# Two reorderings while the first half's expert places are found: raw-weight squares go behind a step's weight copy on ACT, and the sums of gathered rows go behind the pair's filling work on DVE

## The chip, the cores and the metric

The kernel runs on one core of one Trainium2 chip. The metric is the device time of one execution in microseconds, as the median of several runs. Five engines work beside each other, each through its own queue in order: PE (matrix multiplies), ACT (activations and copies), DVE (vector work), POOL (here above all the issue of gathers) and SP (issue of DMAs).

## What is computed

Cut to what matters, the reference adds an attention block and a mixture of very many small experts to the input:

```python
xn = layernorm(x)                                   # 2048 tokens x 512
# A: 32 heads of 16 channels with one shared key and value head
q = (xn @ wq).reshape(B, S, H, Dh); k = xn @ wk; v = xn @ wv
p = softmax(q k^T * Dh**-0.5);  A = (p v).reshape(B, S, H * Dh) @ wo
# B: 32 heads find 2 of 4096 experts for each token
q = einsum("nd,dhc->nhc", xn, w_q)                  # 2 x 128 channels per head
s1 = q[..., :dk] @ k1.T;  s2 = q[..., dk:] @ k2.T   # 64 scores each
# the best 2 of s1 and the best 2 of s2 make 4 candidates, the best 2 are kept
g = softmax(top_s)
act = gelu(einsum("nd,nhkd->nhk", xn, u[top_e]))
B = einsum("nhk,nhk,nhkd->nd", g, act, v[top_e])
out = x + A + B
```

## The kernel before, in words

The 2048 tokens are four groups of 512. For the first two groups ("phases" 0 and 1) the expert rows are fetched by gathers, for the last two a dense form is used that the change does not touch.

**The attention drives the order.** After a start of some 120 us, `att_steps` (L1434 on) is called for each of 256 pairs `d` of key blocks and writes out, in this order: the score matmuls of one key block (`sc`, L452) with their exponentials on ACT (`pt`, L459, two activations of 128x1024), the value matmuls of the pair before (`pv`, L469), then `mid()`, then the score matmuls and exponentials of the second key block, then `fill()`. The two `sc` tiles in PSUM are a pair: a score matmul waits until ACT has read the tile two places back.

**`fill()`** takes as much as fits of the thread that finds the places of the experts (`run_scores`, `score_thread`). For each of 8 blocks `c` of four heads this thread (1) forms weights in `wp_make(c)`: four `pw` products (L648), copied by ACT to `wt` (L649), then for each of four `k` four transposes into a tile `pwt`, one ACT activation that writes the high half `wk` (L663 before, L661 after) and one DVE operation that writes the low half (`low`, L664); and (2) scores the four token tiles in `item`: twelve `psc` matmuls (L720), eight MAX on DVE (L733) and four index searches (L740). `pw`, `pwt`, `psc` and a few small products share three PSUM tiles of the tag "x": a new one starts when DVE or ACT has read the tile that leaves.

The raw weights of the block that comes next must have a size factor. `wp_square` (L619, ACT, 128x1024 with an accumulated sum of squares) is called four times for each block, in `wp_make` at `k` = 1 (two), 2 and 3 (one each). The sums of squares go through `wp_factors` (product `pn` on PE, `xw` on ACT, three small DVE operations at L223 to L225 into `cols`), before the next block's copies use them.

**`mid()`** holds the work on gathered rows of phase 0 and 1. A step writes out some 2.6 gathered rows each of:
- dots (L1243, DVE): the row's first half times the token, summed;
- after each fourth dot, a chain of three small DVE operations, `gq` (L1252), `gy` (L1253) and `ga` (L1254), kept in the list `CHAIN`;
- the tanh of such four dots on ACT (`gth<-gy`, L1259), written at the start of the next step's `mid()`, so between the two pairs of exponentials;
- `weigh` (`w`, L1266, DVE), which needs the tanh;
- sums (L1278, DVE, `xa<-g,w,xa`): the row's second half, weighted, added to the token's total. They are written by `go()`, mixed with the chain and with other small work;
- `gathers(4)`, also in `go()`: up to four more gathers (L1231, issued by POOL) into the 12 row buffers that the sums have set free; and stores of finished totals.

In the kernel before `go()` runs inside `mid()`, unless `dense_on[0] == 2`; then it is put in the list `POST_FILL`, which `fill()` runs after `run_scores`, and `CHAIN` is run beforehand, inside `mid()`.

`IDX` holds one entry for each token tile and block whose places are known; phase 0 fills it with `NC * TPH` = 32 entries. In the profile this stretch ends at 356 us.

Of the kernel before, what the change touches and what calls it, by code (L numbers as in the profile page):

```python
# [33 lines left out]
NC = 8  # L34
TPH = GT
# [26 lines left out]
def tile_kernel(ctx, tc, exact, flag, x, wq, wkv, wo, wqT, kT, uv, ub, vb, out):  # L62
# [538 lines left out]
    def wp_load(c, h):  # L601
        n = 4 * c + h
        if n < 2 or n > 7 and (n - 8) % 5 < 2:
            w = big.tile([P, 2, D], F32, name="wqt", tag="wqt", bufs=2)
        elif n < 8:
            w = gtile(F32, (P, 2, D), "wqt")
        else:
            w = late[0].tile([P, 2, D], F32, name="wqt", tag="gy", bufs=3)
        nc.sync.dma_start(w, wqT[4 * c + h].rearrange("(s p) d -> p s d", p=P))
        WC["raw", c, h] = w  # L610
# [4 lines left out]
    def wp_square():  # L615
        n = squared[0]
        squared[0] += 1
        junk = big.tile([P, 2, D], BF16, name="junk", tag="wk", bufs=NWK)
        nc.scalar.activation(junk, WC["raw", n // 4, n % 4], AF.Square, accum_out=squares[:, n % 4:n % 4 + 1])  # L619

    def wp_factors():
        c = factored[0]
        factored[0] += 1
        p = xtile("pn")[:, :1]
        for h in range(4):
            nc.tensor.matmul(p, ones_f, squares[:, h:h + 1], start=h == 0, stop=h == 3)
        x = small.tile([P, 1], F32, name="xw")
        nc.scalar.activation(x, p, AF.Copy, scale=col(K2))
        factors(x.bitcast(I32), col(S_W + c), col(I_W + c))

    def wk_tile():
        return big.tile([P, 2, 512], F16, name="wk", tag="wk", bufs=NWK)

    def wp_make(c):

        wt = [big.tile([P, 2, 512], F32, name="wt", tag="da", bufs=2) for _ in range(2)]
        for h in range(4):
            for n in range(4 * c + h + 1, min(4 * c + h + 5, 4 * NC) if late[0] else 4):
                if ("raw", n // 4, n % 4) not in WC:
                    wp_load(n // 4, n % 4)  # L640
            if c == 2 and h > 1:
                wp_square()
            if c > 2 and h == 1:
                wp_factors()
            w = WC.pop(("raw", c, h))
            p = xtile("pw")
            for s in range(2):
                nc.tensor.matmul(p[s * E:(s + 1) * E, :], kTs[:, s, :], w[:, s, :], start=True, stop=True)  # L648
            nc.scalar.copy(wt[h // 2][:, h % 2, :], p)  # L649
            yield 0.9  # L650
        WC[c] = []
        if c == 2:
            yield 0.05
            wp_factors()
            yield 0.05
        for k in range(KC):
            for _ in range((0, 2, 1, 1)[k] if 1 < c < NC - 1 else 0):
                wp_square()
            p = xtile("pwt")
            for h in range(4):  # L660
                nc.tensor.transpose(p[:, h * P:(h + 1) * P], wt[h // 2][:, h % 2, k * P:(k + 1) * P], ident)  # L661
            wk = wk_tile()
            nc.scalar.activation(wk[:, 0, :], p, AF.Copy, scale=col(S_W + c))  # L663
            low = lambda p=p, wk=wk: nc.vector.scalar_tensor_tensor(wk[:, 1, :], p, col(S_W + c), wk[:, 0, :],  # L664
                                                                    op0=OP.mult, op1=OP.subtract)
            if c == 1 and late[0] is None:
                AFTER.append(low)
            else:
                low()
            WC[c].append(wk)  # L670
            (store if c > 1 else BULK.append)(lambda k=k, wk=wk: nc.sync.dma_start(d_w[c][:, k], raw(wk[:])))
            yield 0.45
# [72 lines left out]
    IDX, G = {}, {}  # L745
# [516 lines left out]
    def weigh(n):  # L1262
        if n not in WT and n < a_ready[0] // SB:
            ga, th = GA.pop(n), TH.pop(n)
            w = small.tile([P, SB], F32, name="w", bufs=3)
            nc.vector.scalar_tensor_tensor(w, th, 1.0, ga, op0=OP.add, op1=OP.mult)  # L1266
            WT[n] = w
# [23 lines left out]
    def dots(to):  # L1291
        while d_next[0] < min(to, NSL):
            dot(d_next[0])
            d_next[0] += 1
# [7 lines left out]
    def tanhs(to):  # L1302
        while a_ready[0] + SB <= to:
            tanh(a_ready[0] // SB)
            a_ready[0] += SB
# [8 lines left out]
    def run(fns):  # L1314
        todo = fns[:]
        fns.clear()
        for fn in todo:
            fn()
# [92 lines left out]
    dense_on, quiet = [0], [0]  # L1411
# [90 lines left out]
    def score_steps(n):  # L1502
        for _ in range(n):
            spent[0] += next(sgen)
# [122 lines left out]
    with tc.manual_schedule(engines=ENGINES):  # L1627
        nc.vector.tensor_copy(PK["mm"][96:128], PK["mm"][:32])
        run(AFTER)
        score_steps(3)  # L1630
        done0 = spent[0] - 5.4
        half = STEPS // 2
        pos, since = 0.0, half
        for d in range(half + 24):


            if dense_on[0] != 0:
                since = d
            if dense_on[0] == 1:
                pos += 2.35 if d < half * 3 // 4 else max(0.0, NSL - pos) / max(half - 3 - d, 1)  # L1640
            else:
                pos += (2.6 if len(IDX) < NC * TPH else 2.45 if 0 <= d - since < 32 else 2.05, 0, 0.25, 1.5, 0.5)[dense_on[0]]

            todo = max(min(int(pos + 0.001), g_next[0]) - d_next[0], 0) if d else 0

            def mid():
                post = POST[:]
                POST.clear()
                for act, _ in post:
                    act()  # L1650
                tanhs(d_next[0])
                room = ROOM - 0.65 * len(ON_ACT) - 0.7 * len(LAST)
                run(ON_ACT)
                ON_ACT.extend(LATER_ACT)
                LATER_ACT.clear()
                run(LAST)
                while PARTS and (room > 0.7 or len(PARTS) > 3):
                    PARTS.pop(0)()
                    room -= 0.75
                LAST.extend(LATER)  # L1660
                LATER.clear()
                rest = BEHIND[:]
                BEHIND.clear()

                dots(d_next[0] + todo - 1)
                if a_ready[0] > a_next[0]:
                    weigh(a_next[0] // SB)
                dots(d_next[0] + 1 if todo > 0 else 0)
                for _, fn in post:
                    fn()  # L1670
                sums = min(a_ready[0] - a_next[0], max(todo, 3) if d < half else 4)
                if dense_on[0] > 2:
                    sums = min(sums, 2)
                if quiet[0] > 0:
                    quiet[0] -= 1
                    sums = 0
                if dense_on[0] == 2:
                    run(CHAIN)

                def go():  # L1680
                    n = sums
                    while rest or CHAIN or n > 0:
                        if n > 0:
                            adds(1)
                            n -= 1
                        elif not rest:
                            run(CHAIN)
                        if CHAIN:
                            CHAIN.pop(0)()
                        if rest:  # L1690
                            rest.pop(0)()
                    gathers(4)

                    for _ in range(1 if d < half - 4 else NT):
                        if OUTS:
                            experts_out(OUTS.pop(0))

                if dense_on[0] == 2:
                    POST_FILL.append(go)
                else:  # L1700
                    go()

            aim = done0 + (FILL - done0) * (d + 1) / half if d < half else 1e6

            def fill():
                run_scores(until=min(aim, spent[0] + MOST))
                run(POST_FILL)

            norm_steps(d)
            att_steps(d, mid, fill)  # L1710
            if d == half - 26 and not exact:
                met_most()
            if d == half - 16 and not exact:
                met_flag()
        flush()
        run(STORES)
        while a_next[0] < NSL:
            dots(NSL)
            run(CHAIN)
            tanhs(d_next[0])  # L1720
            adds(SB)
            run(STORES)
            gathers(NGB)
        assert not OUTS
        run(STORES)
# [42 lines left out]
```

## Time and profile before

| | |
|---|---|
| median of 3 runs | 1788.83 us (1785.12 to 1790.47) |
| the profiled execution, its own time | 1779.54 us |
| span of that execution | 1777.7 us |
| PE busy | 1692.0 us (95%) |
| DVE busy | 1534.4 us (86%) |
| ACT busy | 1329.0 us (75%) |
| POOL busy | 709.5 us (40%) |
| granted clock of PE, mean | 0.991 |

A row of the timeline has the start in us from the start of the span, the duration in us, the engine, the line, the operation with its output and inputs, a count if several are merged, and in square brackets the idle time of the engine just before, with what ended it. Three matmul rows can overlap by some hundredths, since their ends are modelled. A row of a table by stage has the stretch, its length, and for each engine the busy us and the number of instructions, then the granted clock of PE (1.00 is full), the busy share of the DMA engines and GB/s.

### The profile page before, as it was taken

The numbers are of one execution on the slowest core, as the hardware profiler recorded it, in microseconds if no ns is written. First come the engines' busy times: TensorE is split into PE (matmuls) and PEld (weight loads), VectorE is DVE, ScalarE is ACT, GpSimd is POOL, SyncE is SP. The second block draws the span as 40 slices with busy tenths as digits, with TensorE's granted clock in tenths as the row PEclk, the third lists the DMA queues.
The fourth block names the chain that finished last, engine by engine and source line by source line (L and its number), as shares of the span: only waits on it lengthen the run. The fifth ranks groups of instructions, "written<-read, shape, count | busy, mean of one in ns | idle before, by whom it ended". The sixth has DMA issues, their size and how long they took to land.

```text
span 1777.7 us, 34221 instructions
## 1 busy us (share of the span) xinstructions
PE 1692.0 (95%) x11071; PEld 598.4 (34%) x11071; DVE 1534.4 (86%) x5385; ACT 1329.0 (75%) x1793; POOL 709.5 (40%) x983
## 2 busy tenths in 40 slices
PE   7989998999999889999999999999998999999997
PEld 3433333333333333333333333333333333333332
DVE  7648888989999977988998898999999778888894
ACT  6468787867777988888988666666679877777773
POOL 1024454555663103433433356566640124444430
PEclk9999999999999999999999999999999999999999
DMA  7378888999983469999899977877653779999892
GB/s 263 128 243 310 278 297 286 307 335 337 330 277 138 159 214 296 301 309 320 290 350 318 334 271 250 281 265 255 195 183 111 257 235 291 305 324 313 262 313 70
DMA packets 257277, 471.02 MB, mean 265 GB/s; under 512 B 107316, under 2 KB 118596, under 8 KB 257084
## 3 DMA queue, kind: packets, MB, share of 16 engines
q0 software_dynamic: 73728, 268.47, 43.7%
q1 hardware_dynamic: 182940, 199.59, 34.8%
q8 instruction: 89, 1.46, 0.3%
q14 instruction: 104, 0.85, 0.1%
q10 hardware_dynamic: 416, 0.66, 0.1%
HBM read 407.36 MB, written 56.39 MB: 261 GB/s over the span
## 4 chain that ended last, share of the span: by engine, by line
PE 67%; DVE 15%; ACT 6%; issue 2%; DMA 2%; ACTq 0%; SPq 0%; DVEq 0%
PE pv L469 20%; PE psc L720 13%; PE sc L452 12%; PE pout L1109 9%; PE pact L967 8%; ACT pt L459 4%; DVE xa L1278 2%; PE pwo L569 2%; DVE oh L1025 2%; DVE g L1243 2%; DVE i L740 2%; DVE m L733 2%; PE pw L648 1%; DVE obs L1028 1%; DVE obs L1027 1%
## 5 line engine op out<-in xcount | busy, mean ns | idle before, releaser
L459 ACT ACTIVATE pt<-sc 128x1024 f32<-128x1024 f32 x1024 | 990.2, 1026 | 318.6 <-PE sc L452 317.5
L1231 POOL DMA_INDIRECT g<-in_uv_dram,idx x512 | 546.6, 1068 | 866.6 <-DVE xa L1278 429.9
L469 PE MATMUL pv<-pt,vaug 128*32 128x512 f32 x4096 | 497.8, 604 | 0.0
L1278 DVE SCALAR_TENSOR_TENSOR xa<-g,w,xa 128x512 f32<-128x512 f32 x512 | 372.4, 744 | 0.1
L720 PE MATMUL psc<-wk,xt 128*128 128x512 f16 x1536 | 357.7, 381 | 5.1 <-DVE wk L664 5.1
L452 PE MATMUL sc<-qa,kaug 64*128 64x512 f16 x2048 | 323.5, 383 | 37.7 <-ACT pt L459 33.7
L1243 DVE CUSTOM_DVE_ANT_0 g<-g,xa 128x512 f32<-128x512 f32 x512 | 333.8, 681 | 0.0
L720 PEld LDWEIGHTS <-xt 128*128 128x128 f16 x1536 | 141.2, 98 | 202.7 <-issue 54.1
L452 PEld LDWEIGHTS <-kaug 64*128 64x128 f16 x2048 | 82.1, 94 | 375.3 <-issue 369.3
L469 PEld LDWEIGHTS pv<-pt,vaug 128*32 128x32 f32 x4096 | 107.6, 110 | 255.9 <-issue 255.9
L967 PE MATMUL pact<-xt,wk 128*128 128x512 f16 x768 | 181.5, 381 | 0.0
L1109 PE MATMUL pout<-wk,wd 128*128 128x512 f16 x768 | 175.8, 379 | 0.0
L733 DVE MAX8 m<-psc 128x8 f32<-128x64 f32 x1024 | 145.7, 212 | 18.3 <-PE psc L720 18.2
L740 DVE FIND_INDEX8 i<-m,psc 128x8 uint32<-128x128 f32 x512 | 138.4, 285 | 0.0
L1109 PEld LDWEIGHTS <-wd 128*128 128x128 f16 x768 | 73.0, 98 | 92.5 <-issue 7.9
L967 PEld LDWEIGHTS <-wk 128*128 128x128 f16 x768 | 68.9, 98 | 99.5 <-issue 26.3
L1025 DVE TENSOR_TENSOR oh<-io,tr 128x2048 f16<-128x2048 f16 x64 | 77.8, 1216 | 5.1 <-PE pg L1063 4.8
L1182 DVE SCALAR_TENSOR_TENSOR gy<-gy,pact 128x512 f32<-128x512 f32 x60 | 41.0, 683 | 36.3 <-ACT gy L1181 35.6
L1266 DVE SCALAR_TENSOR_TENSOR w<-gth,ga 128x4 f32<-128x4 f32 x128 | 20.5, 160 | 55.8 <-ACT gth L1259 55.6
L1112 DVE SCALAR_TENSOR_TENSOR da<-pout,cols,da 128x512 f32<-128x512 f32 x72 | 53.4, 745 | 14.5 <-PE pout L1109 14.4
L784 POOL CAST fi<-i 128x32 f32<-128x32 uint32 x60 | 12.6, 240 | 106.3 <-DVE i L740 106.3
L918 DVE SCALAR_TENSOR_TENSOR wk<-rw,cols,wk 128x512 f16<-128x512 f32 x64 | 47.3, 743 | 6.5 <-ACT wk L911 6.5
(238 smaller groups left out, 1499.9 us busy)
## 6 DMA issues: line engine op xcount, KB each, us to landing
wk<-dw SPq DMA_DIRECT2D x96, 256.0 KB
wqt<-in_wqT_dram SPq DMA_DIRECT2D x32, 512.0 KB
un<-in_uv_dram SPq DMA_DIRECT2D x16, 1024.0 KB
ds<-wk SPq DMA_DIRECT2D x64, 256.0 KB
gates<-dg SPq DMA_DIRECT2D x64, 256.0 KB
wk<-ds SPq DMA_DIRECT2D x64, 256.0 KB
dg<-gst SPq DMA_DIRECT2D x14, 928.0 KB
dw<-wk SPq DMA_DIRECT2D x32, 256.0 KB
```

Source lines behind the costliest of these rows:

```text
L452: nc.tensor.matmul(p[:, b, :], kaug[o:o + 64, kc * P:(kc + 1) * P], QA[u][o:o + 64, i, :], start=True, stop=True)
L459: nc.scalar.activation(PT[u, kc, i], p, AF.Exp, scale=SCALE)
L469: nc.tensor.matmul(PV[u][32 * j:32 * j + 32, :], vaug[:, kc, :], pt[:, b, :], start=kc == 0, stop=kc == 15)
L720: nc.tensor.matmul(p, XT[kk][:, a, j * P:(j + 1) * P], WC[n_][kk][:, bb, :], start=n == 0, stop=n == 11)
L733: nc.vector.max(m8[:, jb, s // 2, SECOND * (s % 2):][:, :8], p[:, s * E:(s + 1) * E])
L740: nc.vector.max_index(i8[:, jb, h, :8], m8[:, jb, h, :8], p[:, h * P:(h + 1) * P])
L967: nc.tensor.matmul(p, us[:, a, k * P:(k + 1) * P], XT[k][:, c, :], start=n == 0, stop=n == 11)
L1025: nc.vector.tensor_tensor(out=oa, in0=num(P), in1=bc(0, tb, P), op=OP.is_equal)
L1109: nc.tensor.matmul(p, wd[0][:, a, j * P:(j + 1) * P], vs[:, c, :], start=n == 0, stop=n == last)
L1231: nc.gpsimd.indirect_dma_start(out=gt, out_offset=None, in_=uv, in_offset=bass.IndirectOffsetOnAxis(ap=IDX[ph, c, ti][:, s:s + 1], axis=0))
L1243: nc.vector.tensor_tensor_reduce(u, u, XN[TPH * ph + ti], scale=1.0, scalar=0.0, op0=OP.mult, op1=OP.add, accum_out=a[:, i:i + 1])
L1278: nc.vector.scalar_tensor_tensor(acc, v, w[:, i:i + 1], acc, op0=OP.mult, op1=OP.add)
```

## The change

Two places are edited. In `wp_make` the calls of `wp_square` at a step `k` move from ahead of that step's transposes and `wk` activation to just behind the activation. And as long as `IDX` has fewer than 32 entries, `go()` (sums, chain, other small work, gathers, stores of totals) is not run in `mid()` but put in `POST_FILL`, so it is written behind the filling work of the same step. `CHAIN` is not run ahead in this new case: the condition for that stays `dense_on[0] == 2`.

```diff
@@ wp_make
         for k in range(KC):
-            for _ in range((0, 2, 1, 1)[k] if 1 < c < NC - 1 else 0):
-                wp_square()
             p = xtile("pwt")
             for h in range(4):
                 nc.tensor.transpose(p[:, h * P:(h + 1) * P], wt[h // 2][:, h % 2, k * P:(k + 1) * P], ident)
             wk = wk_tile()
             nc.scalar.activation(wk[:, 0, :], p, AF.Copy, scale=col(S_W + c))
+            for _ in range((0, 2, 1, 1)[k] if 1 < c < NC - 1 else 0):
+                wp_square()
@@ mid
-                if dense_on[0] == 2:
+                if dense_on[0] == 2 or len(IDX) < NC * TPH:
                     POST_FILL.append(go)
                 else:
                     go()
```

No instruction is added or taken out. The orders of PE and SP are the same row for row. Those of ACT, DVE and POOL change. On ACT, in the weight forming that the profile of before shows from 182 to 195 us (`pt` are the exponentials, `junk` the squares, `wk` the weight copies, `gth` a tanh), before:

```order
L663 ACTIVATE wk<-pwt,cols 128x512
L619 ACTIVATE junk,squares<-wqt 128x1024 x2
L663 ACTIVATE wk<-pwt,cols 128x512
L459 ACTIVATE pt<-sc 128x1024 x2
L1259 ACTIVATE gth<-gy 128x4
L459 ACTIVATE pt<-sc 128x1024 x2
L619 ACTIVATE junk,squares<-wqt 128x1024
L663 ACTIVATE wk<-pwt,cols 128x512
L619 ACTIVATE junk,squares<-wqt 128x1024
L663 ACTIVATE wk<-pwt,cols 128x512
L459 ACTIVATE pt<-sc 128x1024 x2
```

The same place after:

```order
L661 ACTIVATE wk<-pwt,cols 128x512 x2
L619 ACTIVATE junk,squares<-wqt 128x1024 x2
L459 ACTIVATE pt<-sc 128x1024 x2
L1259 ACTIVATE gth<-gy 128x4
L459 ACTIVATE pt<-sc 128x1024 x2
L661 ACTIVATE wk<-pwt,cols 128x512
L619 ACTIVATE junk,squares<-wqt 128x1024
L661 ACTIVATE wk<-pwt,cols 128x512
L619 ACTIVATE junk,squares<-wqt 128x1024
L459 ACTIVATE pt<-sc 128x1024 x2
```

Each copy stands one or two squares earlier; the same four copies and four squares stand between the same exponentials.

On DVE, at the place that the profile of before shows from 284 to 293 us (`ISA g,act` with `ISA act` is a dot, `xa` a sum, `gq`, `gy`, `ga` the chain, MAX and MAX_INDEX the reading of a finished `psc` tile), before:

```order
L1243 ISA g,act<-g,xa 128x512
L1243 ISA act 128x1
L1278 SCALAR_TENSOR_TENSOR xa<-g,w,xa 128x512
L1252 SCALAR_TENSOR_TENSOR gq<-act 128x4
L1278 SCALAR_TENSOR_TENSOR xa<-g,w,xa 128x512
L1253 SCALAR_TENSOR_TENSOR gy<-gq,act 128x4
L1278 SCALAR_TENSOR_TENSOR xa<-g,w,xa 128x512
L1254 TENSOR_TENSOR ga<-act,gg 128x4
L733 MAX m_3473<-psc 128x8 x8
L740 MAX_INDEX i_3474<-m_3473,psc 128x8 x4
L664 SCALAR_TENSOR_TENSOR wk<-pwt,cols,wk 128x512 x2
L1243 ISA g,act<-g,xa 128x512
```

and after:

```order
L1243 ISA g,act<-g,xa 128x512
L1243 ISA act 128x1
L733 MAX m_3461<-psc 128x8 x8
L740 MAX_INDEX i_3462<-m_3461,psc 128x8 x4
L664 SCALAR_TENSOR_TENSOR wk<-pwt,cols,wk 128x512 x2
L1278 SCALAR_TENSOR_TENSOR xa<-g,w,xa 128x512
L1252 SCALAR_TENSOR_TENSOR gq<-act 128x4
L1278 SCALAR_TENSOR_TENSOR xa<-g,w,xa 128x512
L1253 SCALAR_TENSOR_TENSOR gy<-gq,act 128x4
L1278 SCALAR_TENSOR_TENSOR xa<-g,w,xa 128x512
L1254 TENSOR_TENSOR ga<-act,gg 128x4
L1243 ISA g,act<-g,xa 128x512
```

The reading of `psc` and the two low halves come ahead of the three sums; the chain with `gy`, from which ACT's next tanh reads, comes behind them.

## The prediction

> **What bounds the kernel now.** I read the page first, then the table of the stretch that the change reaches, PE's timeline there, the granted clock around its gaps, and then ACT and DVE at the same places. From the page:
>
> ```profile
> span 1777.7 us, 34221 instructions
> PE 1692.0 (95%) x11071; PEld 598.4 (34%) x11071; DVE 1534.4 (86%) x5385; ACT 1329.0 (75%) x1793; POOL 709.5 (40%) x983
> PE 67%; DVE 15%; ACT 6%; issue 2%; DMA 2%; ACTq 0%; SPq 0%; DVEq 0%
> ```
>
> PE carries the chain of waits, so an edit that leaves PE's order alone, as this one does, can only change how long PE stands still. The table of the stretch in which phase 0's places are found (us, then PE, PEld, DVE, ACT, POOL busy, granted clock, DMA share):
>
> ```profile
> 131.00:356.00 225.00, 211.73 (x1299) 74.51 (x1300) 193.09 (x865) 179.30 (x262) 109.63 (x153) 0.98 0.87 297
> ```
>
> PE lacks 225.00 - 211.73 = 13.3 us here, 0.75% of the span: the most that waits can give. DVE has 32 us to spare, ACT 45.7. Of the 13.3 us 11.7 stand in these rows of PE's timeline (idle time in brackets):
>
> ```profile
> 152.18 0.39 PE L452 MATMUL sc<-qa,kaug 64*128 64x512 f16 x2 [1.21 <-ACT pt L459]
> 185.76 1.46 PE L720 MATMUL psc<-wk,xt 128*128 128x512 f16 x6 [0.92 <-DVE wk L664]
> 194.43 2.15 PE L720 MATMUL psc<-wk,xt 128*128 128x512 f16 x6 [1.96 <-DVE wk L664]
> 228.50 0.39 PE L452 MATMUL sc<-qa,kaug 64*128 64x512 f16 x2 [1.05 <-ACT pt L459]
> 261.62 0.81 PE L720 MATMUL psc<-wk,xt 128*128 128x512 f16 x3 [1.01 <-DVE wk L664]
> 291.26 0.63 PE L661 MATMUL pwt<-ident,wt 128*128 128x128 f32 x4 [2.35 <-DVE i L740]
> 300.30 1.48 PE L648 MATMUL pw<-wqt,kTs 128*64 128x512 f32 x4 [2.36 <-issue]
> 324.33 0.81 PE L720 MATMUL psc<-wk,xt 128*128 128x512 f16 x3 [0.88 <-DVE wk L664]
> ```
>
> Behind three of these gaps the granted clock falls (columns: stretch, length, PE busy, clock, DMA share, GB/s):
>
> ```profile
> 154.00:156.00 2.00, 2.00 (x9) 0.52 0.81 315
> 156.00:158.00 2.00, 2.00 (x8) 0.63 0.04 13
> 194.00:196.00 2.00, 1.57 (x6) 0.76 0.86 278
> 196.00:198.00 2.00, 2.00 (x10) 0.50 0.96 348
> 300.00:302.00 2.00, 1.70 (x6) 0.71 0.88 311
> 302.00:304.00 2.00, 2.00 (x12) 0.50 0.82 252
> ```
>
> The lost clock is (0.48 + 0.37 + 0.24 + 0.50 + 0.29 + 0.50) x 2 us = 4.8 us, 1.6 us for each dip. The gap of 2.35 us at 291 has no dip behind it, so a gap of about two microseconds brings one sometimes.
>
> [...]
>
> **The change part by part.** *Squares behind the copy.* ACT and DVE around the gap at 194.43:
>
> ```profile
> 191.86 1.06 ACT L619 ACTIVATE junk<-wqt 128x1024 bf16<-128x1024 f32 x1
> 192.90 0.69 ACT L663 ACTIVATE wk<-pwt,cols 128x512 f16<-128x512 f32 x1
> 192.55 0.15 DVE L1254 TENSOR_TENSOR ga<-act,gg 128x4 f32<-128x4 f32 x1
> 193.62 0.75 DVE L664 SCALAR_TENSOR_TENSOR wk<-pwt,cols,wk 128x512 f16<-128x512 f32 x1 [0.92 <-ACT wk L663]
> ```
>
> The copy waits 1.04 us for a square whose result nobody needs yet; DVE's low half waits for the copy, and PE for the PSUM tile that the low half frees. Behind the change the copy starts at 191.86 and, with the sums (the last with `ga` at 192.55) out of DVE's way, the low half at 193.62 - 1.04 = 192.6: I take 1.1 us of the 1.96. Ahead of the gaps at 261.62 and 152.18 stand these:
>
> ```profile
> 259.06 1.06 ACT L619 ACTIVATE junk<-wqt 128x1024 bf16<-128x1024 f32 x1
> 147.88 0.69 ACT L663 ACTIVATE wk<-pwt,cols 128x512 f16<-128x512 f32 x1 [1.79 <-DVE cols L225]
> ```
>
> The first is again a square ahead of a copy, with its low half and PE behind: 0.8 of 1.01 us, since DVE comes a little later there. In the second ACT waits 1.79 us for `cols`, which moves ahead of three sums on DVE, so the exponentials that PE waits for come sooner: 0.9 of 1.21 us. At 185.76 and 324.33 neither a square nor a sum is in front, and the gaps stay. The work of ACT between two pairs of exponentials is as much as before, so the gap at 228.50 stays too. The squares themselves are read by `pn` steps later; a microsecond there is nothing.
>
> *Sums behind the fill.* PE and DVE ahead of the gap at 291.26, and DVE ahead of that at 300.30:
>
> ```profile
> 286.35 0.82 PE L720 MATMUL psc<-wk,xt 128*128 128x512 f16 x3
> 286.70 0.75 DVE L1278 SCALAR_TENSOR_TENSOR xa<-g,w,xa 128x512 f32<-128x512 f32 x1
> 288.10 0.15 DVE L1253 SCALAR_TENSOR_TENSOR gy<-gq,act 128x4 f32<-128x4 f32 x1
> 288.91 1.14 DVE L733 MAX8 m<-psc 128x8 f32<-128x64 f32 x8
> 298.00 1.14 DVE L733 MAX8 m<-psc 128x8 f32<-128x64 f32 x8
> ```
>
> `psc` is finished at 287.1, but its reading starts at 288.91, since three sums with the chain (286.70 to 288.91) are first. Behind the change it starts at 287.1: 1.8 us of the 2.35 go. At 298.00 the same, less what DVE is later there because the sums of the step before now stand behind its reading: I take 1.6 of 2.36. PE's gaps shrink by 1.1 + 0.8 + 0.9 + 1.8 + 1.6 = 6.2 us. Of the dips I give back half, 2.4 of 4.8 us, since some gap is left at each place; the ends are 0 and 4.8.
>
> *The new wait.* The chain moves with the sums, and ACT's tanh, which reads `gy`, does not. A step with its rows on PE, DVE and ACT:
>
> ```profile
> 164.05 1.47 PE L720 MATMUL psc<-wk,xt 128*128 128x512 f16 x6
> 165.21 0.17 DVE L1253 SCALAR_TENSOR_TENSOR gy<-gq,act 128x4 f32<-128x4 f32 x1
> 165.94 1.94 ACT L459 ACTIVATE pt<-sc 128x1024 f32<-128x1024 f32 x2 [1.19 <-PE sc L452]
> 167.69 0.67 DVE L1243 CUSTOM_DVE_ANT_0 g<-g,xa 128x512 f32<-128x512 f32 x1
> 167.77 0.21 ACT L1259 ACTIVATE gth<-gy 128x4 f32<-128x4 f32 x1
> ```
>
> Today `gy` is there 2.4 us before ACT comes to the tanh. `psc` is finished only at 165.5, so the reading can't come sooner; behind it, from 167.69, stand a sum, `gq`, a sum and `gy`, 1.6 us by the rows quoted above (286.70 to 288.10 + 0.15). The tanh then starts at 169.3 and ACT has waited 1.5 us, with the second pair of exponentials queued behind. The groups of all these tanhs and of the exponentials in the stretch, with their idle time:
>
> ```profile
> L1259 ACT ACTIVATE gth<-gy 128x4 f32<-128x4 f32 x19 | 4.0, 210 | 0.0
> L459 ACT ACTIVATE pt<-sc 128x1024 f32<-128x1024 f32 x122 | 118.2, 1025 | 27.2 <-PE sc L452 27.0
> ```
>
> None of the 19 tanhs waits today; 19 x 1.5 = 28.5 us of ACT's time is the most. The 122 exponentials are those of 30 steps. In a light step ACT has the room (45.7 us idle, 1.5 for each step). It has little in the steps with squares, two in each of five blocks: 10 of 30 steps, with 19 x 10/30 = 6.3 tanhs. Of each wait ACT's usual gap ahead of a pair of exponentials, 27.2/61 = 0.45 us, takes its part, and 6.3 x 1.05 = 6.7 us pass to PE. The ends are 0 (DVE reads `psc` so early that `gy` is in time) and 14 us (half of all waits pass). That a held-up ACT stops PE is seen once in the trace, at 384:
>
> ```profile
> 382.80 1.06 ACT L1379 ACTIVATE un<-un 128x1024 f32<-128x1024 f32 x1 [4.17 <-DMA un<-in_uv_dram]
> 383.85 3.75 ACT L459 ACTIVATE pt<-sc 128x1024 f32<-128x1024 f32 x4
> 384.91 0.39 PE L452 MATMUL sc<-qa,kaug 64*128 64x512 f16 x2 [2.36 <-ACT pt L459]
> ```
>
> 4.17 us of waiting became 2.36 us of PE's.
>
> *Gathers* are issued by POOL half a step later, with their sums. I cost that at nothing: 12 buffers hold more than two steps of rows, and the dots, on the whole kernel, never waited for one (idle 0.0):
>
> ```profile
> L1243 DVE CUSTOM_DVE_ANT_0 g<-g,xa 128x512 f32<-128x512 f32 x512 | 333.8, 681 | 0.0
> ```
>
> If that cover went, the idle time of this group would show it, and half a step of delay, about 3 us, is the most for one row.
>
> **The sum.** -6.2 - 2.4 + 6.7 = -1.9 us: the profiled execution would come to 1779.54 - 1.9 = 1777.6 us. It lay 9.3 us under the median of the runs; the same step from the median is 1786.9 us. About 0.3%, 5.4 us, is what a measurement of this kernel can tell from no change.
>
> **The rivals.** *The tanh's wait is hidden.* For it speaks ACT's idle time of 45.7 us, and that DVE, which today stands before `w` until the tanh is done, then has the reading of `psc` to do; against it, that the copies of the next weights follow on ACT. The gain would be 6.2 + 2.4 = 8.6 us: 1780.2, faster.
>
> *The tanh's wait wins.* ACT, held at each tanh, gives its exponentials late, and PE stands at `sc`. With 14 us passed on, 6.2 us of gaps gone and no dip saved it is 1788.83 + 7.8 = 1796.6, slower. It decides as soon as more than 6.2 + 2.4 + 5.4 = 14.0 us pass, or 11.6 if the dips stay. For it speaks that all 19 tanhs get the new wait; against it, that 20 of 30 steps have room.
>
> *The gain is swallowed at 384.* ACT waits there for rows that a DMA brings. If their landing does not move with PE, the 1.9 us are spent there: 1788.8. Against it speaks that the load is issued in PE's rhythm.
>
> *The dips do not hang on these gaps.* Then the clock falls elsewhere in the same measure and only waits count: -6.2 + 6.7 = 0.5, 1789.3. Against it speaks that each of the three dips begins at a gap; for it, that the gap at 291 brought none. [...]
>
> **How the numbers follow.** My forecast has 0.40, swallowed 0.08, dips independent 0.08: together 0.56 within 0.3% of the median. Tanh hidden has 0.30, the chance of faster; tanh wins 0.14, the chance of slower. The range runs from 1778 (hidden, and nearly all the clock back: 6.2 + 4.6 = 10.8 us) to 1794 (9.5 us passed on, half of the gaps' and the dips' share had: 9.5 - 3.1 - 1.2 = 5.2 us), which leaves out the far ends of both rivals.
>
> **What would show it.** In the profile after: the gaps at 194, 291 and 300 shrunk under 1.2 us, those at 186 and 324 as they were; a new row "ACT gth waits for DVE gy" with 10 to 28 us over some 19 tanhs; PE's wait for `pt` in the stretch grown by some 4 to 8 us; and one or two dips instead of three. I am wrong if `gth` does not wait, if the long gaps stay, or if the time moves outside 131 to 356 us by more than a few microseconds.

## The result, and the profile after

The changed kernel takes 1806.04 us (median of 6 runs, 1800.83 to 1810.18), the kernel before 1788.24 us (median of 6 runs beside it). The ratio is 1.0113, with a 95% interval of 1.0092 to 1.0133: about 20 us slower. Ratios here leave out single slow executions, among them one of 2418.94 us of the kernel before in this comparison and one of 5813.61 us in an experiment below. The forecast was 1786.9 us, no change, with a range that ended at 1794.

The profiled execution of the changed kernel took 1810.18 us, the slowest of its six. Two groups of its page stand out against before, where the dots' group (L1243) had an idle time of 0.0 and the score matmuls' group (L452) waited 33.7 us for `pt`:

```profile
span 1808.5 us, 34225 instructions
PE 1701.8 (94%) x11071; PEld 600.1 (33%) x11071; DVE 1537.2 (85%) x5385; ACT 1327.7 (73%) x1793; POOL 715.8 (40%) x983
PE 61%; DVE 17%; ACT 7%; issue 4%; DMA 2%; another core or an unknown queue 1%; SPq 1%; ACTq 0%; DVEq 0%
...
L452 PE MATMUL sc<-qa,kaug 64*128 64x512 f16 x2048 | 327.9, 384 | 59.5 <-ACT pt L459 47.5
...
L1243 DVE CUSTOM_DVE_ANT_0 g<-g,xa 128x512 f32<-128x512 f32 x512 | 335.0, 683 | 17.1 <-DMA g<-in_uv_dram,idx 14.5
```

PE's share of the chain of waits fell from 67% to 61%, and PE is busy for only 10 us more in a span that is 31 us longer: the rest is PE standing still. The page's groups are of the whole kernel. The stretch of the change holds the same work as 131 to 356 us before (122 exponentials, 19 tanhs) when it is read from 131 to 372 us. Its row of the table by stage, and then its groups:

```profile
131.00:372.00 241.00, 215.57 (x1301) 75.78 (x1297) 194.56 (x867) 178.63 (x262) 114.06 (x156) 0.97 0.83 280
```

```profile
L1259 ACT ACTIVATE gth<-gy 128x4 f32<-128x4 f32 x19 | 4.0, 208 | 22.1 <-DVE gy L1253 11.3 <-DVE gg L815 6.5 <-issue 4.2
L1243 DVE CUSTOM_DVE_ANT_0 g<-g,xa 128x512 f32<-128x512 f32 x78 | 51.2, 687 | 14.5 <-DMA g<-in_uv_dram,idx 14.5
L452 PE MATMUL sc<-qa,kaug 64*128 64x512 f16 x240 | 39.6, 389 | 15.8 <-ACT pt L459 9.9 <-issue 3.3 <-DMA xt<-dxt 2.6
L720 PE MATMUL psc<-wk,xt 128*128 128x512 f16 x345 | 86.8, 387 | 4.6 <-DVE wk L664 4.6
L1266 DVE SCALAR_TENSOR_TENSOR w<-gth,ga 128x4 f32<-128x4 f32 x19 | 2.9, 153 | 0.9 <-ACT gth L1259 0.9
```

The stretch grew by 241 - 225 = 16 us. PE is idle for 241.00 - 215.57 = 25.4 us of it, before 13.3: 12.1 us more. The tanhs wait 22.1 us (before 0.0), the dots 14.5 us for rows that a DMA brings (before 0.0), and PE's idle time ahead of `sc` went from 3.5 to 15.8 us. PE's gaps of over 0.8 us, where eight stood before:

```profile
175.62 0.39 PE L452 MATMUL sc<-qa,kaug 64*128 64x512 f16 x2 [1.77 <-issue]
177.06 0.39 PE L452 MATMUL sc<-qa,kaug 64*128 64x512 f16 x2 [1.05 <-issue]
189.06 1.46 PE L720 MATMUL psc<-wk,xt 128*128 128x512 f16 x6 [0.92 <-DVE wk L664]
196.72 1.45 PE L720 MATMUL psc<-wk,xt 128*128 128x512 f16 x6 [0.96 <-DVE wk L664]
231.62 0.39 PE L452 MATMUL sc<-qa,kaug 64*128 64x512 f16 x2 [2.88 <-ACT pt L459]
258.66 0.81 PE L720 MATMUL psc<-wk,xt 128*128 128x512 f16 x3 [0.87 <-DVE wk L664]
307.47 1.98 PE L648 MATMUL pw<-wqt,kTs 128*64 128x512 f32 x4 [3.50 <-issue]
331.71 0.81 PE L720 MATMUL psc<-wk,xt 128*128 128x512 f16 x3 [1.30 <-DVE wk L664]
353.94 0.39 PE L452 MATMUL sc<-qa,kaug 64*128 64x512 f16 x2 [1.26 <-ACT pt L459]
363.57 0.47 PE L452 MATMUL sc<-qa,kaug 64*128 64x512 f16 x2 [2.59 <-DMA xt<-dxt]
```

The gap at 291 is down to 0.67 us and those at 152 and 194 shrank. In their place stand gaps at `sc`, where PE waits for the exponentials, and the gap of 2.36 us at 300 has become 3.50. How the largest wait of a tanh comes about, in the timeline of POOL, DVE, ACT and PE:

```profile
351.81 1.18 POOL L1231 DMA_INDIRECT g<-in_uv_dram,idx  x1 [0.30 <-DVE ga L1254]
...
356.36 0.69 DVE L1243 CUSTOM_DVE_ANT_0 g<-g,xa 128x512 f32<-128x512 f32 x1 [4.10 <-DMA g<-in_uv_dram,idx]
356.98 1.15 DVE L733 MAX8 m<-psc 128x8 f32<-128x64 f32 x8
...
359.76 0.16 DVE L1252 SCALAR_TENSOR_TENSOR gq<-act 128x4 f32<-128x4 f32 x1
...
361.18 0.15 DVE L1253 SCALAR_TENSOR_TENSOR gy<-gq,act 128x4 f32<-128x4 f32 x1
...
361.37 0.21 ACT L1259 ACTIVATE gth<-gy 128x4 f32<-128x4 f32 x1 [4.74 <-DVE gg L815]
...
362.52 2.83 ACT L459 ACTIVATE pt<-sc 128x1024 f32<-128x1024 f32 x3
...
363.57 0.47 PE L452 MATMUL sc<-qa,kaug 64*128 64x512 f16 x2 [2.59 <-DMA xt<-dxt]
```

A dot waits 4.10 us for its row, the reading of `psc` follows it, and only behind the reading and two sums comes `gy`. The tanh waits 4.74 us for it; behind the tanh stand another activation of 1.04 us (`un`, L1379) and then the exponentials, and PE is idle until the first of these has read its tile (the profile names a DMA as the releaser of 363.57; an experiment below makes the same gap with ACT alone). Of the three longest waits of a tanh only this one has a late row ahead of it; the next two, 2.77 us at 351 and 2.19 us at 224, have none. The pair of gaps at 175 and 177 us has no releaser that the profile names and no waiting tanh just ahead; its cause stays open.

Where the profiled execution falls behind before, by the start of ACT's copies of `pv` (L477, one for each unit of attention; the start after less the start before):

| start before, us | 175 | 236 | 295 | 353 | 511 | 857 | 1118 | 1758 |
|---|---|---|---|---|---|---|---|---|
| after | +2.2 | +4.5 | +5.9 | +15.2 | +19.5 | +19.7 | +28.6 | +31.3 |
| squares alone | -1.0 | -3.6 | -1.9 | -1.9 | -3.7 | -4.0 | -5.3 | -5.0 |

By 511 us 19.5 us are lost, near the difference of the medians (17.8 us). The steps that follow later are no part of it: the step between 1066 and 1118 us also stands, with 3 to 4 us, in two controls below that are no slower than before, and executions of the changed kernel lie up to 9 us apart. So verdicts come from ratios, and a profile says where PE stands.

### The profile page after: what moved, and what is told of

It is laid out like the page before. It is cut to its first block, busy times and chain, and to the rows that moved or that the text cites. A ratio compares the mean times of both kernels' runs of the same rounds, so it can differ in the third digit from the quotient of the medians.

```text
span 1808.5 us, 34225 instructions
## 1 busy us (share of the span) xinstructions
PE 1701.8 (94%) x11071; PEld 600.1 (33%) x11071; DVE 1537.2 (85%) x5385; ACT 1327.7 (73%) x1793; POOL 715.8 (40%) x983
## 4 chain that ended last, share of the span: by engine, by line
PE 61%; DVE 17%; ACT 7%; issue 4%; DMA 2%; another core or an unknown queue 1%; SPq 1%; ACTq 0%; DVEq 0%
PE pv L469 18%; PE sc L452 11%; PE psc L720 11%; PE pout L1109 8%; PE pact L967 8%; ACT pt L459 5%; DVE xa L1278 3%; PE pwo L569 2%; DVE i L740 2%; DVE m L733 2%; DVE g L1243 2%; DVE oh L1025 2%; PE pw L648 1%; DMA xt<-dxt 1%
## 5 line engine op out<-in xcount | busy, mean ns | idle before, releaser
L452 PE MATMUL sc<-qa,kaug 64*128 64x512 f16 x2048 | 327.9, 384 | 59.5 <-ACT pt L459 47.5
L1243 DVE CUSTOM_DVE_ANT_0 g<-g,xa 128x512 f32<-128x512 f32 x512 | 335.0, 683 | 17.1 <-DMA g<-in_uv_dram,idx 14.5
L452 PEld LDWEIGHTS <-kaug 64*128 64x128 f16 x2048 | 83.9, 94 | 406.4 <-issue 398.0
L1112 DVE SCALAR_TENSOR_TENSOR da<-pout,cols,da 128x512 f32<-128x512 f32 x72 | 53.5, 747 | 14.5 <-PE pout L1109 12.7
```

Of the source, the lines that this page charges most:

```text
L452: nc.tensor.matmul(p[:, b, :], kaug[o:o + 64, kc * P:(kc + 1) * P], QA[u][o:o + 64, i, :], start=True, stop=True)
L1243: nc.vector.tensor_tensor_reduce(u, u, XN[TPH * ph + ti], scale=1.0, scalar=0.0, op0=OP.mult, op1=OP.add, accum_out=a[:, i:i + 1])
```

## Theories

T: ACT, held at the tanh by a late `gy`, gives its exponentials late, and PE pays at `sc`. That is the rival "the tanh's wait wins" of the prediction, at a higher price. G: gathers, issued half a step later, bring their rows late, and dots that wait for them hold up what stands behind them on DVE. The prediction costed that at nothing.

## The experiments

Ratios are to the kernel before, measured beside each; the intervals are 95%.

**Squares alone** (the first half of the diff).

> Only the squares go behind the copies; the sums, the chain and the gathers stay where they are in the kernel before. Theory T (the time is lost because the tanh on ACT waits for gy, and the exponentials stand behind it) and theory G (the time is lost because gathers are issued half a step later, so that dots on DVE wait for rows) both put the loss on the other edit. Both expect 0.997 to 1.001 of the kernel before, dots idle 0.0, no tanh that waits for gy. A ratio over 1.004 would put part of the loss on the squares, against both.

Measured: 0.9997 (0.9976 to 1.0019). The gap at 194 shrank from 1.96 to 0.95 us and the one at 261 fell under 0.7, as forecast for these two; less than 2 us is too little to be seen in the time.

```profile
192.40 1.46 PE L720 MATMUL psc<-wk,xt 128*128 128x512 f16 x6 [0.95 <-DVE wk L664]
```

**Sums alone** (the second half of the diff).

> Only the sums, the chain and the gathers go behind the fill; the squares stay ahead of the copies. T and G both expect nearly the whole loss of the changed kernel, 1.010 to 1.014 of the kernel before, with some 11 us of tanhs waiting for gy and some 14 us of dots waiting for gathers. A ratio under 1.006 would mean that the two edits are worse together than apart.

Measured: 1.0097 (1.0065 to 1.0130); tanhs wait 26.1 us, dots 15.6. The loss lies in this half, as both theories had it.

**Chain ahead**: both edits, and

```diff
-                if dense_on[0] == 2:
+                if dense_on[0] == 2 or len(IDX) < NC * TPH:
                     run(CHAIN)
```

> Both edits, but the chain (gq, gy, ga) is run ahead, in mid, so that the tanh has its input as early as in the kernel before; sums and gathers stay behind the fill. T expects the loss to be gone: 0.997 to 1.002 of the kernel before, PE's wait for pt back near its 33.7 us. G expects most of it to stay: 1.006 to 1.011, with 10 us or more of dots waiting for gathers, and tanhs that wait only because their dots were late.

Measured: 1.0036 (1.0017 to 1.0055). Up to 356 us the tanhs wait 2.2 us and the dots 23.2. Two thirds of the loss went with the tanhs' wait, though the dots wait longer than in the changed kernel; one third stayed. Neither theory is the whole. But T isn't wholly out of this run: just behind 356 us, where the old order comes back, a tanh waits 4.60 us, and PE with it:

```profile
364.25 0.20 ACT L1259 ACTIVATE gth<-gy 128x4 f32<-128x4 f32 x1 [4.60 <-DVE gy L1253]
366.65 0.39 PE L452 MATMUL sc<-qa,kaug 64*128 64x512 f16 x2 [3.09 <-ACT pt L459]
```

**Chain behind, sums and gathers where they were**: the squares' edit, and in `mid`

```diff
-                    while rest or CHAIN or n > 0:
+                    while rest or CHAIN and not apart or n > 0:
...
-                        if CHAIN:
+                        if CHAIN and not apart:
...
+                    if apart:
+                        POST_FILL.append(lambda: run(CHAIN))
```

with `apart = len(IDX) < NC * TPH`.

> Squares behind the copies, sums and gathers in mid as in the kernel before, and the chain alone behind the fill. T expects tanhs that wait for gy (some 5 us in sum, less than in the changed kernel since no sums stand before gy) and 1.001 to 1.005 of the kernel before. G expects 0.997 to 1.001: the gathers are issued as early as in the kernel before, and the dots are idle 0.0.

Measured: 0.9988 (0.9965 to 1.0011). The tanhs wait only 3.4 us, since no sum stands ahead of the chain behind the reading. The ratio is what G forecast, and only the end of its interval touches T's range. A dose this small costs nothing that can be seen, so it hardly tells the theories apart.

**Chain first behind the fill**: both edits, and `go` begins with `run(CHAIN)` in the new case, so sums no longer stand ahead of `gy`, but the reading does.

> Both edits as in the changed kernel, but behind the fill the chain stands first, ahead of the sums and gathers. Gathers are as late as in the changed kernel and as with the chain ahead. Theory T (ACT held at the tanh is the price, late gathers only one reason for a late gy) expects a dose between those two: tanhs waiting 9 to 16 us in sum and 1.004 to 1.008 of the kernel before. Theory G (late gathers are the price) expects no difference to the changed kernel that the chain's place could make, and since that was refuted in its strong form by the run with the chain ahead (1.0036), its weak form expects 1.0036 again, whatever the tanhs wait.

Measured: 1.0042 (1.0027 to 1.0058); tanhs wait 10.0 us, dots 18.1. It is within T's range, but also within the interval of the run with the chain ahead: what separates this kernel from the changed one is the sums between reading and `gy`.

**ACT held evenly, and in lumps**: the kernel before, with small activations put ahead of tanhs (five ahead of each; then 25 ahead of each fifth).

```diff
+                if len(IDX) < NC * TPH and a_ready[0] + SB <= d_next[0]:
+                    n = a_ready[0] // SB
+                    for _ in range(5):
+                        nc.scalar.activation(HELD, ident[:, :SB], AF.Copy)
                 tanhs(d_next[0])
```

> The kernel before, with five additional small activations (128x4) on ACT ahead of each of the 20 tanhs in phase 0, about 1 us each time and 20 us in sum, near the 22.1 us that the tanhs waited in the changed kernel; no edit of the change is in. T expects that a hold of this sum costs much of the loss wherever it comes from: 1.004 to 1.009. The prediction's reckoning (two of three steps have room, 6.7 of 28.5 us pass) expects 24% of 20 us, 5 us, 1.002 to 1.004.

> As the run with ACT held evenly, but 25 small activations ahead of every fifth tanh: four holds of some 5 us, the same sum of 20 us. If what passes to PE depends on the sum alone, this costs what the even hold costs, within 0.2%. If it depends on the length of the single hold (one pair of exponentials of room, then PE stands, and the clock dips behind it), each lump makes a gap of 2.5 to 3.5 us at sc and a dip of 1.6 us: 16 to 20 us, 1.009 to 1.011.

Measured: evenly 1.0026 (1.0007 to 1.0044), in lumps 1.0118 (1.0098 to 1.0139). The added activations of the even holds, as a group of the stretch (those of the lumps are as many and sum to 20.5 us):

```profile
L1655 ACT ACTIVATE held<-ident 128x4 f32<-128x4 f32 x100 | 20.6, 206 | 2.5
```

The same 20.5 us of ACT cost 0.26% or 4.6 us of the kernel in holds of 1 us (1.2 to 7.8 by the interval) and 1.18% or 21 us in holds of 5. Of the even holds 22% pass (6 to 38% by the interval), beside the 24% of the prediction; what T had expected of them, 0.4 to 0.9%, is missed. One lump on ACT and PE:

```profile
175.94 4.94 ACT L1655 ACTIVATE held<-ident 128x4 f32<-128x4 f32 x21
180.78 0.19 ACT L1260 ACTIVATE gth<-gy 128x4 f32<-128x4 f32 x1
180.88 1.92 ACT L459 ACTIVATE pt<-sc 128x1024 f32<-128x1024 f32 x2
181.93 0.39 PE L452 MATMUL sc<-qa,kaug 64*128 64x512 f16 x2 [3.15 <-ACT pt L459]
```

Of this hold of 5 us 3.15 reach PE; some two microseconds are hidden, about as long as a whole even hold and more. One thing differs from the changed kernel: here `w` on DVE, which needs the tanh, stands ahead of the reading and waits too (30.5 us in lumps, 21.5 evenly, 0.9 in the changed kernel), so a part of these prices came over DVE: PE's two longest gaps in the lumps' run are not at `sc` but at `pw` (8.15 us at 319) and at `psc` (5.67 us at 247). The next run has no such path.

**Waits replayed**: the run with the chain ahead, in which `w` stands behind the fill, with as many small activations ahead of each tanh as make up its wait in the changed kernel.

> The run with the chain ahead (1.0036), in which the tanhs hardly wait, with small activations (128x4, 0.206 us each) ahead of each tanh on ACT, as many as make up the time that the same tanh waited in the changed kernel: 0.84, 0.58, 1.83, 0, 0.40, 1.35, 1.13, 2.19, 0, 1.72, 0.46, 1.52, 1.17, 0, 0, 0.31, 1.04, 2.77 and 4.74 us. T expects the changed kernel's loss to come back, 1.009 to 1.013, since ACT is held as long and in the same places. If the loss between the two runs came from the chain's place on DVE in another way than over the tanh, it stays at 1.003 to 1.006.

Measured: 1.0085 (1.0059 to 1.0111), against 1.0036 without the holds. Its gaps at `sc` are nearly those of the changed kernel, though no tanh waits for `gy`:

```profile
227.83 0.61 PE L452 MATMUL sc<-qa,kaug 64*128 64x512 f16 x2 [2.93 <-ACT pt L459]
...
351.56 0.39 PE L452 MATMUL sc<-qa,kaug 64*128 64x512 f16 x2 [1.31 <-ACT pt L459]
361.65 0.68 PE L452 MATMUL sc<-qa,kaug 64*128 64x512 f16 x2 [3.05 <-DMA xt<-dxt]
```

In the changed kernel they are 2.88, 1.26 and 2.59 us at 231.62, 353.94 and 363.57. Holding ACT as long in the same places brings back these gaps and, by the ratios, some two thirds of the 0.77% between the two runs; the ratio falls just short of the 1.009 that T gave as its lower end.

**Tanh behind the exponentials**: the changed kernel, with the tanh written behind the second pair of exponentials of its step (`w` goes to the sums with it; `done` counts the dots whose tanh is due).

```diff
-                tanhs(d_next[0])
+                if apart:
+                    PRE_FILL.append(lambda: tanhs(ready))
+                else:
+                    tanhs(ready)
...
             def fill():
+                run(PRE_FILL)
                 run_scores(until=min(aim, spent[0] + MOST))
```

> The changed kernel, chain, sums and gathers behind the fill as there, and only the tanh moved on ACT: behind the second pair of exponentials of its step, ahead of the copies of the filling work, so that no exponential stands behind a tanh that waits for gy (w goes with it, to the sums). T expects most of the loss to be gone: 1.001 to 1.005, about what the run with the chain ahead gave. If the loss came from the late chain or the late gathers in another way, 1.009 to 1.013 as in the changed kernel.

Measured: 1.0044 (1.0024 to 1.0065). Chain, sums and gathers are as in the changed kernel; on ACT one operation of 0.2 us moved, and 0.7 of the 1.13% are gone. The dots still wait 16.9 us, and of the pair of gaps at 175 us one of 1.99 us is still there. With the replay this shows T from both sides.

**13 and 11 row buffers**, for what is left with the chain ahead (0.36%). `NGB` is 13 (with `NWK` 12 for 14, which makes room) or 11; the controls have the squares' edit alone.

> The run with the chain ahead, with 13 row buffers for 12; the place for it comes from the weights' buffers, 12 for 14. One more row in flight is 2.7 us of lead for each gather (7 us for a step of 2.6 rows). G in its weak form (what is left of the loss, 0.36%, is dots that wait for late gathers) expects the dots' wait to fall from 25.8 us to under 5 and the time to within 0.15% of the control with the same buffers. The rival, that what is left comes from the order on DVE itself, expects the dots' wait to fall and the time to stay 0.3% above the control.

> The control for the run with 13 row buffers: squares behind the copies, all else as in the kernel before, 13 row buffers and 12 weight buffers. Both expect that a kernel whose dots never waited gains nothing from a 13th buffer: 0.998 to 1.003 of the kernel before, the upper end if the two weight buffers are missed.

Measured: 1.0083 (1.0056 to 1.0110) with the chain ahead, 1.0002 (0.9981 to 1.0023) for the control. The dots' wait fell to 3.3 us, yet the time rose. Its profile has stalls of PE that have no wait of a dot or a tanh ahead of them (2.94 us at 180, 4.99 us at 387, put down to "issue" and `pt`). Neither theory had this; the pair settles nothing on G, and why it is slow stays open.

> The run with the chain ahead, with 11 row buffers for 12. One row fewer in flight makes each gather later by another third of a step. G in its weak form (what is left with the chain ahead, 0.36%, comes from dots that wait for late gathers and stand ahead of the reading of psc) expects the dots' wait to grow from 25.8 us to 40 or more and 0.3 to 0.8% above the control with 11 buffers and 1.006 to 1.012 of the kernel before. The rival (the order of sums and fill itself, not the gathers) expects 1.002 to 1.005 of the control whatever the dots wait.

> The control with 11 row buffers: squares behind the copies, all else as in the kernel before. Both expect that a lead of 14 us in the median, less 2.7 us for one row, is still over the 6 us that a gather needs: dots idle under 5 us, 0.998 to 1.003 of the kernel before.

Measured: 1.0118 (1.0090 to 1.0145) with the chain ahead, 0.9974 (0.9961 to 0.9988) for the control, so 1.4% apart. With 11 buffers and the chain ahead, in the stretch (131 to 375 us):

```profile
L1243 DVE CUSTOM_DVE_ANT_0 g<-g,xa 128x512 f32<-128x512 f32 x77 | 50.8, 687 | 39.3 <-DMA g<-in_uv_dram,idx 35.3 <-issue 3.9
L720 PE MATMUL psc<-wk,xt 128*128 128x512 f16 x345 | 87.7, 390 | 10.6 <-DVE wk L664 10.6
L1259 ACT ACTIVATE gth<-gy 128x4 f32<-128x4 f32 x20 | 4.2, 210 | 2.5 <-DVE gy L1253 2.5
```

Here the tanhs hardly wait (2.5 us; with 12 buffers 6.8 in the same window, 4.60 of it at 364 us), and the dots wait 39.3 us (23.2 with 12 buffers). PE pays at `psc` and `pw`, which need what DVE does behind such a dot. In the same run, ahead of PE's gap at 310.99:

```profile
307.73 0.69 DVE L1243 CUSTOM_DVE_ANT_0 g<-g,xa 128x512 f32<-128x512 f32 x1 [1.60 <-DMA g<-in_uv_dram,idx]
...
308.69 1.14 DVE L733 MAX8 m<-psc 128x8 f32<-128x64 f32 x8
...
310.99 1.98 PE L648 MATMUL pw<-wqt,kTs 128*64 128x512 f32 x4 [4.93 <-issue]
```

This shows G as a mechanism with a dose: the 1.4% are more than the 0.3 to 0.8% that it forecast, and the rival's 0.2 to 0.5% is out. It makes G the likely cause of a good part of the 0.36% that 12 buffers leave; the tanh at 364 us has a share in those that no run separates. The control with 11 buffers is the only version below before, by 0.26%; that is under the 0.3% that the prediction set as its bound.

## Why the prediction was wrong

In the prediction's own terms: PE's idle time in the stretch was to go down by 6.2 us at five gaps and up by 6.7 us for the tanhs. The five gaps gave 2.9 us (those at 152, 194, 261 and 291 gave 4.0, that at 300 took 1.1), and as the whole grew by 12.1 us, PE's other gaps grew by 15.0. The dips of the clock, from which 2.4 us were to come back, cost 1.7 us more. Two steps failed.

**The gathers, costed at nothing.** The prediction took "12 buffers hold more than two steps of rows" for cover, with the dots' idle time of 0.0 as witness. Idle 0.0 says that the cover lasts, not how much is left of it. It could have been read from the same trace: from the end of the n-th gather's issue on POOL to the start of the n-th dot there were 13.7 us in the median over the 76 dots that start in the stretch, but 5.5 us at the least, and a row took 4.3 to 9.2 us from the start of its issue to landing (20 gathers of the stretch have a landing in the trace). After the change the lead is 10.6 us in the median and 3.3 at the least. Half of the 12 buffers hold rows that have had their dot and wait for their sum: by 250 us 54 gathers had been issued, 49 dots and 43 sums begun, so the cover was 5 rows, not 12. The waits are of the size that the prediction named as the most (about 3 us; the longest is 4.10), but they pass on, over what stands behind the dot on DVE. With the tanhs out of the way the prediction's sum is its rival "hidden", a gain of 8.6 us; the run with the chain ahead, where they hardly wait up to 356 us, lost 6.4 us (3.0 to 9.8). There the two gaps that were to shrink by 1.8 and 1.6 us are 2.69 and 3.36 us long. So late rows took the gains and more; how much of these 15 us is theirs alone is not measured. In the changed kernel they also make the longest wait of a tanh, 4.74 us.

**The tanh's term, 6.7 us, was mis-sized.** Its sum was near: 22.1 us over 19 tanhs, forecast 28.5 at most; in part that is luck, since the largest wait came from a late row that the forecast did not have. Its share that passes fits even waits (22% measured, with a wide interval and a part over DVE; 24% forecast). What failed is that all waits were given one length, 1.5 us. They are 0 to 4.74 us, and what passes hangs on the single wait. Between the changed kernel and the two runs that relieve the tanh lie 0.7 to 0.8%, 12 to 14 us; the replay gives back 0.5%. So the term was 12 to 14 us where the sum had 6.7. That is the "14 us (half of all waits pass)" of the prediction's upper end, and the point from which its rival decided.

**The gains came in part.** The gaps at 194 and 261 fell nearly as forecast (squares), to 0.96 and 0.54 us. The gap at 152 fell from 1.21 to 0.36 us and that at 291 from 2.35 to 0.67. The one at 300, forecast to lose 1.6 us, grew by 1.1: a dot that waits 2.14 us for its row stands there ahead of the reading.

```profile
304.54 0.69 DVE L1243 CUSTOM_DVE_ANT_0 g<-g,xa 128x512 f32<-128x512 f32 x1 [2.14 <-DMA g<-in_uv_dram,idx]
305.16 1.15 DVE L733 MAX8 m<-psc 128x8 f32<-128x64 f32 x8
```

The gap at 228 was said to stay; it went from 1.05 to 2.88 us, by a tanh that waited 2.19 us in a step with squares. There the prediction had the right place for the wait to pass, and no price for a long one.

**The clock.** Instead of one or two dips there are four, each behind a gap or a pair of gaps of 2.6 to 3.5 us, at 175, 231, 307 and 363 us. Read from where it starts, each dip lasts 3.41 us at a clock of 0.50, so it costs 1.7 us. The prediction's 1.6 us and 4.8 us leave out the ends of the dips, which its stretches of 2 us miss: its three cost 5.1 us. The four after cost 6.8 us, 1.7 more. Here they are, each with the 3.41 us ahead of it (stretch, length, busy PE, PEld, DVE, ACT and POOL, clock, DMA share, GB/s):

```profile
173.98:177.39 3.41, 0.72 (x5) 0.20 (x4) 2.17 (x8) 2.05 (x2) 1.96 (x2) 1.00 1.00 396
177.39:180.80 3.41, 3.41 (x10) 1.02 (x10) 0.63 (x5) 2.52 (x4) 0.00 (x0) 0.50 1.03 403
228.59:232.00 3.41, 0.53 (x6) 0.19 (x3) 2.34 (x15) 3.41 (x7) 0.00 (x0) 1.00 0.89 301
232.00:235.41 3.41, 2.89 (x11) 1.55 (x10) 3.27 (x14) 3.41 (x5) 2.49 (x6) 0.50 0.72 273
303.68:307.09 3.41, 0.28 (x2) 0.00 (x0) 2.55 (x18) 1.38 (x3) 0.16 (x1) 1.00 0.94 320
307.09:310.51 3.42, 3.04 (x12) 0.63 (x16) 3.28 (x16) 1.01 (x2) 2.76 (x9) 0.50 0.44 142
361.71:365.12 3.41, 1.11 (x8) 0.38 (x11) 3.41 (x18) 3.41 (x5) 2.08 (x2) 1.00 1.11 289
365.12:368.53 3.41, 3.41 (x20) 0.57 (x12) 3.31 (x27) 1.43 (x3) 0.25 (x2) 0.50 0.95 320
```

So of the 16 us by which the stretch grew 12.1 are waits of PE and 1.7 clock; 2.2 us are in neither. The dips moved with the gaps, as the forecast had it and the rival did not.

**What would show it** read rightly where it named the tanh's waits (10 to 28 us) and PE's wait for `pt` (grown by 6.4 us in the stretch, 4 to 8 forecast), but those came with gaps that the profile put down to other releasers ("issue", a DMA), 5.9 us at `sc` alone. And the aftermath counts: some 4 of the 19.5 us were lost between 356 and 511 us, outside the stretch, which the prediction had named as a sign against it.

## What to carry to other kernels

When work that frees buffers is moved later, read how long before its use the scarcest transfer is issued, the least and not the mean, and compare it with its time to land; an idle time of zero says nothing about the margin (here it stood beside a lead of 5.5 us at the least and rows that took up to 9.2 us to land). A wait that is put on an in-order queue is priced by its longest cases: what lies within the queue's usual slack is nearly free, and here much of what went beyond it passed on (of holds of 1 us 22% reached PE, of a hold of 4.94 us 3.15). Where a small operation with a late input stands ahead of the work that feeds the bounding engine, move that small operation, not the work; here that took back 0.7 of the 1.13%, and not the rest.

## What was not expected of the hardware

The length of a gap doesn't settle whether the granted clock falls behind it. In the changed kernel the gap of 2.88 us at 231.62 brought a dip to 0.50. In the run with the chain ahead a gap of 3.36 us did not:

```profile
300.22 1.08 PE L648 MATMUL pw<-wqt,kTs 128*64 128x512 f32 x4 [3.36 <-issue]
```

What differs between the two in the traces is how the idle time lies against the times at which dips begin. In the changed kernel the four dips of the stretch begin at 177.39, 232.00, 307.09 and 365.12 us, which are 16, 22 and 17 times 3.41 us apart, the length of one dip; in the kernel before the three begin at 154.08, 195.04 and 300.85 us, 12 and 31 times 3.41 us apart. Read in stretches of this length, counted from the dips, PE's idle time ahead of the dip at 232.00 is 3.41 - 0.53 = 2.88 us, all in one stretch. In the run with the chain ahead I take the boundaries from the matmuls that run slowly between 288.65 and 291.92 us (three of `psc` take 1.49 us at 289.53, where three take 0.82 at 294.31). The gap of 3.36 us then leaves 1.82 and 1.54 us in two stretches, and the clock stays at 1.00:

```profile
295.27:298.68 3.41, 1.59 (x9) 0.62 (x7) 1.69 (x11) 2.77 (x5) 0.62 (x1) 1.00 0.92 317
298.68:302.09 3.41, 1.87 (x12) 0.50 (x16) 3.27 (x20) 0.75 (x2) 1.58 (x6) 1.00 0.34 127
302.09:305.50 3.41, 3.41 (x28) 1.19 (x20) 2.84 (x7) 3.15 (x5) 3.19 (x7) 1.00 0.94 247
```

The gap of 2.35 us at 291 in the kernel before, which the prediction found without a dip, is split in the same way, into 1.71 us and 0.65:

```profile
287.20:290.61 3.41, 1.70 (x10) 0.72 (x8) 3.41 (x20) 3.41 (x7) 2.28 (x3) 1.00 0.89 281
290.61:294.02 3.41, 2.76 (x23) 1.22 (x27) 2.53 (x8) 3.04 (x6) 0.88 (x1) 1.00 0.90 281
```

In the traces of the kernel before and of the changed one, of these stretches at full clock from 20 us on, all 18 with more than 1.78 us idle have a dip behind them and none with less than 1.60 has; between the two both occur (1.73 us ahead of the dip at 154.08; 1.78 us from 351.47 us in the changed kernel, without one). In the run with the chain ahead the 1.82 us above have none. So in these two traces PE needn't stand idle through a whole stretch of 3.41 us for the clock to fall behind it. Why the dips lie at these times no run shows.
